# Rows of a routed expert layer turned by DMA transposes instead of by TensorE, from a scratch tensor kept as planes of 16-bit halves

## The chip, the cores and the metric

The kernel runs on one core of a Trainium2 chip, in one launch. The metric is device time in microseconds (us), the median of several executions; less is better. The core has TensorE (PE: matmuls, and PEld, its weight loads), VectorE (DVE), ScalarE (ACT), GpSimd (POOL), SyncE (SP, which here only issues transfers) and 16 DMA engines, which serve the transfers of all queues. SBUF is the working memory of 128 partitions, PSUM the memory of eight banks into which TensorE writes, HBM the main memory. Each engine takes its instructions in order.

## The reference

```python
X = np.fft.rfft(x, axis=1)                   # x: (8, 2496, 256) float32
y = np.fft.irfft(X * (filt_r + 1j * filt_i)[None], n=2496, axis=1)
x = y.reshape(19968, 256)                    # the 19,968 rows
logits = x @ w_gate
noisy = logits + np.log1p(np.exp(x @ w_noise)) * noise
top2 = np.argpartition(-noisy, 2, axis=1)[:, :2]     # 2 of 8 experts for each row
top2_w = softmax of the two noisy logits
for e in range(8):
    for k in range(2):
        mask = top2[:, k] == e
        h = np.maximum(x[mask] @ w1[e], 0.0)         # 256 -> 1024
        out[mask] += top2_w[mask, k, None] * (h @ w2[e])   # 1024 -> 256
```

## The kernel before, in words

The work has two streams that one program interleaves. `fft_stream` filters the eight batches one after the other, as matmuls with small DFT matrices (steps `s1`, `kg0` to `kg2`, `t3`, `i2`), and finds the two experts of each row and their weights (`gate`, `route`). Its last step `i2` (L505 on) brings a chunk of 4 groups of rows by 128 columns from PSUM to the tile `yt` with an ACT copy (L524) and writes it to the scratch tensor `y` in HBM with a DMA on SP's queue (L528). A row of `y` has 256 float32 values and 8 weights, one for each expert.

`expert` (L1069 on) takes the rows in parts of up to 512, all of one expert. For a part, `gather` (L985) fetches the rows from `y` with indirect DMAs on POOL's queue, 128 rows at a time (L993), into one of eight slots `xg` of the tile `stage`. `turn` (L999) turns them, so that the 256 columns lie on partitions: four TensorE transposes of 128 x 128 for each of the two column halves, with the identity as the moving operand, into the PSUM bank `xps` (L1009). ACT rounds the result to a coarse part `mxh` (L1013), DVE computes the rest `mxl` (L1014). The products are made from such pairs, coarse times coarse plus two mixed terms. The first layer is eight groups `f` of six matmuls of 512 columns (L121 to L123, into a bank of tag `hps`, every third one of tag `yps`); ACT and DVE make the pair `hh`, `hl` of each group (L1096, L1097). The second layer goes by row tiles `t` of 128, 16 matmuls each into a bank of tag `yps` (L1121 and L1122 with both halves of the weights side by side, once the batches are far enough, else L121 to L123); ACT and DVE scale the result (L1126, L1128), and an indirect DMA on POOL's queue adds it to `out` (L1129). The weights come by DMAs on SP's queue (`load_w`, L1030 for most) into four slots, and are split into pairs by ACT and DVE (`wsplit`, L1058, L1059). `front` starts the loads of a new expert's weights and calls `turn`.

The order of a part: first layer; then `turn` of the next part, whose rows were fetched by then; then the four tiles of the second layer, with `fetch` ahead of them for the part after the next. So the transposes stand between first and second layer on TensorE, which the FFT steps fill as well. `run` sets how many FFT steps go between the parts (`PACE`, `PACES`). The parts come in sets, one for each batch that is ready: `FIRST` counts parts with weights of their own (2 in all after the first batch, 12 after the second), `PAIRS` pairs of parts that share the weights (1, 6, 11, 16, 21, 26 in all after batches 3 to 8). At the end stand 7 single parts, 14 parts of 256 rows and 4 of 128. This makes 89 parts with 316 row tiles in the run. `pin` writes down the order of the instructions of some steps on their engines; the rest is ordered by the compiler's own schedule. The first two batches are filtered by a plan of slots (`plan`, in `fft_stream`), in which the `i2` of the first batch stand in slots 12 to 17.

## Time and profile before

| | |
|---|---|
| time, median of 3 runs | 2307.39 us (2306.23 to 2309.88) |
| profiled execution, its own time | 2308.6 us |
| its span in the trace | 2306.8 us |
| granted TensorE clock in it | 0.993 |
| TensorE matmul busy | 2253.9 us |
| DVE / ACT / POOL busy | 1540.0 / 1183.1 / 925.5 us |
| bytes moved by DMA | 328.58 MB |

The profile lists instructions by line of the kernel, engine and operation, with the tile written and the tiles read (`xps<-ident,stage` is a transpose of gathered rows into the bank `xps`), how often it ran, how long it was busy in all and in the mean, and how long the engine idled before it and for whom. Records of matmuls overlap, since they are pipelined: what a matmul costs is read from the distance of starts in the timeline, not from its own length. The table of windows gives, for a stretch of time, the busy time of each engine with the number of instructions, then the granted clock (PEclk), the share of time in which the 16 DMA engines were busy, and the rate. The chain of work is followed back from the last instruction to what released it, step by step, and its shares say what the span consists of.

### The profile page before, as it was taken

What the parts mean: (1) busy time and instruction counts of PE and PEld (TensorE: products, weight loads), DVE (VectorE), ACT (ScalarE), POOL (GpSimd) and SP (SyncE); (2) the same over time, 40 slices, a digit from 0 to 9 for tenths busy, and PEclk for the clock granted to TensorE, in tenths of its full rate; (3) what the DMA queues carried; (4) which work ended last, traced back from release to release, by engine and by line L of the source; (5) the groups of instructions that cost most, each with busy time, mean ns of one, the idle gap of its engine ahead of it and who ended that gap; (6) DMA issues with size and microseconds to landing.
All of it is one profiled execution on the core that took longest, in us unless ns stands there. A gap on an engine that the chain in (4) does not pass through costs nothing.

```text
span 2306.8 us, 39164 instructions
## 1 busy us (share of the span) xinstructions
PE 2253.9 (98%) x13023; PEld 1888.2 (82%) x13023; DVE 1540.0 (67%) x3348; ACT 1183.1 (51%) x2369; POOL 925.5 (40%) x819
## 2 busy tenths in 40 slices
PE   8889999999999999999999999999999999999998
PEld 5448888888788888888888888888888888889997
DVE  4767797687669765875659655964444445557886
ACT  6655655654554554444544444444344444546775
POOL 4014253343334333443344433435454544444442
PEclk9989999999999999999999999999999999999999
DMA  8686757755655555454544553444444444657774
GB/s 239 178 255 188 199 141 195 177 149 135 171 137 126 140 140 129 103 144 118 118 114 106 137 142 85 91 99 89 96 92 91 90 98 105 149 138 233 218 215 130
DMA packets 283957, 328.58 MB, mean 142 GB/s; under 512 B 37243, under 2 KB 196963, under 8 KB 283747
## 3 DMA queue, kind: packets, MB, share of 16 engines
q1 hardware_dynamic: 222435, 241.60, 34.5%
q0 software_dynamic: 61312, 84.40, 21.6%
q8 instruction: 104, 1.70, 0.3%
q14 instruction: 106, 0.87, 0.1%
HBM read 221.44 MB, written 105.25 MB: 142 GB/s over the span
## 4 chain that ended last, share of the span: by engine, by line
PE 89%; DMA 4%; DVE 3%; ACT 2%; issue 1%; SPq 1%; POOL 0%; POOLq 0%; ACTq 0%; DVEq 0%
PE yps L1121 21%; PE hps L121 12%; PE hps L122 12%; PE hps L123 12%; PE yps L1122 10%; PE xps L1009 3%; PE q L428 2%; PE yps L123 2%; PE yps L121 2%; PE yps L122 2%; PE q L492 1%; PE u L439 1%; DMA stage<-w 1%; DMA x<-x 1%; PE q L317 1%
## 5 line engine op out<-in xcount | busy, mean ns | idle before, releaser
L1121 PE MATMUL yps<-w,hh 128*128 128x512 f32 x2080 | 737.6, 399 | 0.6 <-DVE stage L1128 0.6
L1129 POOL DMA_INDIRECT out<-stage,ids x316 | 524.8, 1661 | 291.2 <-DVE stage L1128 116.9
L993 POOL DMA_INDIRECT stage<-y,ids x316 | 324.0, 1025 | 623.7 <-PE xps L1009 247.1
L1122 PE MATMUL yps<-w,hl 128*128 128x256 f32 x2080 | 563.3, 280 | 0.1
L1097 DVE SCALAR_TENSOR_TENSOR hl<-hps,hh 128x512 fp32r<-128x512 f32 (+2 forms) x712 | 435.0, 626 | 153.7 <-ACT hh L1096 151.9
L122 PE MATMUL hps<-mxl,w1h 128*128 128x512 f32 (+2 forms) x1424 | 533.0, 375 | 0.0
L121 PE MATMUL hps<-mxh,w1h 128*128 128x512 f32 (+2 forms) x1424 | 524.1, 378 | 1.7 <-DVE hl L1097 1.4
L123 PE MATMUL hps<-mxh,w1l 128*128 128x512 f32 (+2 forms) x1424 | 525.0, 370 | 0.0
L1096 ACT ACTIVATE hh<-hps 128x512 fp32r<-128x512 f32 (+2 forms) x712 | 377.7, 550 | 247.2 <-PE hps L123 241.7
L1121 PEld LDWEIGHTS yps<-w,hh 128*128 128x128 f32 x2080 | 384.2, 188 | 80.4 <-DVE stage L1128 0.9
L1122 PEld LDWEIGHTS yps<-w,hl 128*128 128x128 f32 x2080 | 391.1, 188 | 19.9 <-DVE mxl L1014 1.2
L121 PEld LDWEIGHTS hps<-mxh,w1h 128*128 128x128 f32 x1424 | 265.1, 188 | 50.5 <-DVE hl L1097 3.7
L123 PEld LDWEIGHTS hps<-mxh,w1l 128*128 128x128 f32 x1424 | 268.4, 188 | 45.5
L122 PEld LDWEIGHTS hps<-mxl,w1h 128*128 128x128 f32 x1424 | 268.3, 188 | 40.4 <-issue 0.2
L1126 ACT ACTIVATE stage<-yps,gt 128x256 f32<-128x256 f32 x316 | 142.3, 476 | 281.1 <-PE yps L1122 256.7
L1128 DVE SCALAR_TENSOR_TENSOR stage<-yps,gt,stage 128x256 f32<-128x256 f32 x260 | 119.4, 479 | 184.5 <-ACT stage L1126 184.1
L1014 DVE TENSOR_TENSOR mxl<-xps,mxh 128x512 fp32r<-128x512 f32 (+2 forms) x178 | 112.1, 630 | 149.1 <-ACT mxh L1013 147.0
L1013 ACT CAST mxh<-xps 128x512 fp32r<-128x512 f32 (+2 forms) x178 | 95.9, 539 | 203.3 <-PE xps L1009 170.3
L1058 ACT CAST w1h<-stage 128x512 fp32r<-128x512 f32 x180 | 111.8, 621 | 99.8 <-PE hps L122 52.1
L1059 DVE TENSOR_TENSOR w1l<-stage,w1h 128x512 fp32r<-128x512 f32 x180 | 123.7, 687 | 55.5 <-ACT w1h L1058 54.6
L965 POOL CAST ids<-lt 128x8 int32<-128x8 f32 (+3 forms) x63 | 16.2, 257 | 336.2 <-DMA lt<-lst 330.1
L1059 DVE TENSOR_TENSOR w<-stage,w 128x512 fp32r<-128x512 f32 x216 | 142.4, 686 | 7.9 <-ACT w L1058 7.4
(222 smaller groups left out, 3082.4 us busy)
## 6 DMA issues: line engine op xcount, KB each, us to landing
stage<-w SPq DMA_DIRECT2D x396, 256.0 KB
x<-x SPq DMA_DIRECT2D x88, 256.0 KB
fd<-c SPq DMA_DIRECT2D x77, 240.0 KB
wb<-w SPq DMA_DIRECT2D x18, 1024.0 KB
fx<-fd SPq DMA_DIRECT2D x140, 128.0 KB
out<-z SPq DMA_DIRECT2D x24, 702.0 KB
y<-yt SPq DMA_DIRECT2D x40, 248.6 KB
y<-yt SPq DMA_DIRECT2D x40, 234.0 KB
```

The lines of the kernel that those rows point to most:

```text
L121: nc.tensor.matmul(o, lh, rh, start=start, stop=False)
L122: nc.tensor.matmul(o, lh, rl, start=False, stop=False)
L123: nc.tensor.matmul(o, ll, rh, start=False, stop=stop)
L993: self.pin(lambda: self.nc.gpsimd.indirect_dma_start(out=x, out_offset=None, in_=self.y[:BLK + ready * ROWS], in_offset=bass.IndirectOffse ...
L1059: nc.vector.tensor_sub(l, sv, f32v(h))
L1096: nc.scalar.activation(h, p, AF.Relu)
L1097: nc.vector.scalar_tensor_tensor(l, p, 0.0, f32v(h), op0=ALU.max, op1=ALU.subtract)
L1121: nc.tensor.matmul(bank, h, hl, start=(f == 0), stop=False)
L1122: nc.tensor.matmul(p, l, hl[:, 0], start=False, stop=(f == 7))
L1126: nc.scalar.activation(o, p, AF.Copy, scale=gate[:, t])
L1128: nc.vector.scalar_tensor_tensor(o, bank[:, 1], gate[:, t], o, op0=ALU.mult, op1=ALU.add)
L1129: a = nc.gpsimd.indirect_dma_start(out=self.io["out"][:BLK + ready * ROWS], out_offset=bass.IndirectOffsetOnAxis(ap=ids[:, t:t + 1], axis= ...
```

## The change

- `y` becomes a tensor of 32-bit words in which each 128-column half of a row is stored as 128 low 16-bit halves and then 128 high ones. In `i2`, the ACT copy from PSUM to `yt` goes by 16-bit halves and sorts them so (1024 elements per partition and chunk in place of 512). For the first batch the float32 rows go as before to a tensor `y0` of their own, and POOL makes the planes in a second tile `yp` (tags of `x` and `a`); `yput` writes those to `y`, 12 chunks and one transfer of the weights, in the slots of the plan ahead of the next `i2`. `init_dram` zeroes the pad rows of `y0` too.
- Parts of the set after the first batch (2 parts, 8 row tiles) are gathered from `y0` and turned by TensorE as before. All later parts are gathered from `y`, and `flip` turns each row tile with one DMA transpose of 128 x 512 16-bit elements on SP's queue, into the tile `xt`. `flip` is called after group `f == 1` of the first layer (what is left), and after the second and the fourth tile of the second layer (two row tiles each; all that are there for smaller parts), each time scheduled behind the ACT instruction just issued. `turn` then has two DVE copies of 2 x 512 16-bit elements that put the halves together again as float32 in two slots `x32`, ordered behind the last `hl` of the first layer; L1013 and L1014 follow, and read SBUF in place of PSUM.
- The weights of the rows (`gt`, a POOL copy) are taken when a part's transposes have been issued (`take`), no longer in `turn`. The slots `xg` are 4 in place of 8, those of the scaled results 4 in place of 6. A next part is fetched ahead of the first layer only if the one before it has been flipped.
- The third bank of the first layer has the tag `xps` in place of `yps` for all parts but those of the first set.
- `FIRST` becomes 2, 12, 16: after the third batch four single parts in place of one pair. `PAIRS` becomes 4, 9, 14, 19, 24 after batches 4 to 8. The number of parts stays 89. `PACE` of that third set is 60 in place of 40, and the stream may run a batch further ahead in it.
- The tiles `uh` and `oh` of the gating share buffers with others.

```diff
-FIRST = [_sure(2 * S, BLK), 12]
+FIRST = [_sure(2 * S, BLK), 12, 16]
+ALONE = len(FIRST)
...
-PACE = {0: 110, 1: 200, 2: 40}
+PACE = {0: 110, 1: 200, 2: 60}
...
-        self.y = self.dp.tile([NROW, YW], F32, name="y")
+        self.y = self.dp.tile([NROW, YW], I32, name="y")
+        self.y0 = self.dp.tile([BLK + ROWS, YW], F32, name="y0")
...
+        if n < 2:
+            nc.scalar.copy(yt[:, :k, :128], p[:RP, :m].rearrange("p (g d) -> p g d", g=k))
+            y0 = self.y0[BLK:].rearrange("(p g) d -> p g d", p=RP)[:, g0:g0 + k]
+            nc.sync.dma_start(y0[:, :, h * 128:h * 128 + w], yt[:, :k, :w])
+            yp = P.tile([RP, 4, 128], F32, name="yp", tag="xa"[g0 // 4 % 2], bufs=2)
+            nc.gpsimd.tensor_copy(yp.bitcast(U16)[:, :k].rearrange("p g (two d) -> p g two d", two=2),
+                                  yt.bitcast(U16)[:, :k, :256].rearrange("p g (d two) -> p g two d", two=2))
+            self.yp.append((y[:, :, h * 128:h * 128 + 128], yp.bitcast(I32)[:, :k]))
...
+        nc.scalar.copy(yt.bitcast(U16)[:, :k, :256].rearrange("p g (two d) -> p g two d", two=2),
+                       p.bitcast(U16)[:RP, :2 * m].rearrange("p (g d two) -> p g two d", g=k, two=2))
+        nc.sync.dma_start(y[:, :, h * 128:h * 128 + w], yt.bitcast(I32)[:, :k, :w])
...
+    def flip(self, count, late=None):
+        ent = next((e for e in self.ahead if len(e[3]) < len(e[2][0])), None)
+        if ent is None or ent[0][5] == 1 or self.standing not in (None, ent):
+            return
+        self.standing = ent
+        xg, done = ent[2][0], ent[3]
+        if not done:
+            ent[4] = self.P.tile([128, 4, 512], U16, name="xt", bufs=1)
+        with self.after(late):
+            for t in range(len(done), min(len(done) + count, len(xg))):
+                done.append(self.nc.sync.dma_start_transpose(ent[4][:, :, 128 * t:128 * t + 128], xg[t].bitcast(U16)[:, :2 * D]))
+        if len(done) == len(xg):
+            ent[5] = self.take(ent)
...
+        if ent[0][5] > 1:
+            self.flip(nt)
+            q = [self.slot("x32") for _ in range(2)]
+            for kc in range(2):
+                with self.after(self.lastl):
+                    nc.vector.tensor_copy(q[kc].bitcast(U16)[:, :2 * w].rearrange("p (t two) -> p two t", two=2), ent[4][:, 2 * kc:2 * kc + 2, :w])
+            self.standing = None
...
+            third = ("xps", 1) if ready > 1 else ("yps", 2)
...
+                if f == 1:
+                    self.flip(4, e)
...
+                if t % 2 or nt == 1:
+                    self.flip(2 if nt == 4 else 4, e)
```

More of the change, by code (lines that the diff above doesn't have):

```diff
@@ L615, in fft_stream @@
                     at(o, self.t3, *R[i + 1])
+                if b == 0 and (i == 0 or o > last):
+                    at(o, self.yput)
+                last = o
                 at(o, self.i2, *R[i])
+            if b == 0:
+                at(o + 1, self.yput)
         for j in range(11):
@@ L980, in front @@
             fill()
-        if fill and self.held_any:
-            xT = self.pin(self.turn, xg, nt, hold=False, only=[self.nc.tensor.engine])
+        if fill and self.held_any and ready == 1:
+            xT = self.pin(self.turn, ent, hold=False, only=[self.nc.tensor.engine])
         else:
-            xT = self.turn(xg, nt)
+            xT = self.turn(ent)
         return w1, xT, w2st
     def gather(self, blk, i):
+        nc = self.nc
         lt, n, nt, s, tabi, ready = blk
+        if i == 0:
+            self.ra = nc.gpsimd.value_load(tabi[0:1, 1, s:s + 1], min_val=0, max_val=E - 1)
         xg = []
@@ L992, in gather @@
             x = self.slot("xg")
-            self.pin(lambda: self.nc.gpsimd.indirect_dma_start(
-                out=x, out_offset=None, in_=self.y[:BLK + ready * ROWS],
+            o, y = (x, self.y0) if ready == 1 else (x.bitcast(I32), self.y[:BLK + ready * ROWS])
+            self.pin(lambda: nc.gpsimd.indirect_dma_start(
+                out=o, out_offset=None, in_=y,
                 in_offset=bass.IndirectOffsetOnAxis(ap=lt[:, i, t:t + 1], axis=0)),
-                hold=False, only=[self.nc.gpsimd.engine])
+                hold=False, only=[nc.gpsimd.engine])
@@ L997, in gather, with take @@
             xg.append(x)
-        return xg, self.turns["xg"] + 1 - nt
-    def turn(self, xg, nt):
-        nc, P = self.nc, self.P
+        return xg, self.turns["xg"] + 1 - nt, self.ra
+    def take(self, ent):
+        xg, at, ra = ent[2]
+        gate = self.P.tile([128, 4, 1], F32, name="gt", bufs=3)[:, :len(xg)]
+        rows = self.stage[:, 2048:2048 + 4 * YW].rearrange("p (s w) -> p s w", w=YW)[:, at:at + len(xg), D:]
+        self.nc.gpsimd.tensor_copy(gate, rows[:, :, bass.ds(ra, 1)])
+        return gate
@@ L1005, in turn @@
-        w = 128 * nt
         for kc in range(2):
-            q = self.PS.tile([128, 512], F32, name="xps", bufs=1)
-            for t in range(nt):
-                nc.tensor.transpose(q[:, t * 128:(t + 1) * 128], xg[t][:, kc * 128:(kc + 1) * 128], self.ident)
+            if ent[0][5] > 1:
+                x = q[kc]
+            else:
+                x = self.PS.tile([128, 512], F32, name="xps", bufs=1)
+                for t in range(nt):
+                    nc.tensor.transpose(x[:, t * 128:(t + 1) * 128], xg[t][:, kc * 128:(kc + 1) * 128], self.ident)
@@ L1084, in expert @@
             ids, gate = lt[:, i], xT[2]
-            self.fetch(may)
+            if not self.ahead or len(self.ahead[0][3]) == len(self.ahead[0][2][0]):
+                self.fetch(may)
+            third = ("xps", 1) if ready > 1 else ("yps", 2)
             hh = []
             for f in range(8):
-                p = self.PS.tile([128, 512], F32, name="hps", tag="hps" if f % 3 < 2 else "yps", bufs=2)[:, :w]
+                tag, bufs = ("hps", 2) if f % 3 < 2 else third
+                p = self.PS.tile([128, 512], F32, name="hps", tag=tag, bufs=bufs)[:, :w]
                 for kc in range(2):
@@ L1105, in expert @@
             if self.ahead:
-                b2, i2, x2 = self.ahead[0]
-                cur = (w1, self.turn(x2, nt), None) if i2 else self.front(b2, x2, fill if late else None)
+                e2 = self.ahead[0]
+                cur = (w1, self.turn(e2), None) if e2[1] else self.front(e2, fill if late else None)
             self.fetch(may)
```

78 lines of the change are left out of this document (43 added, 35 removed).

## Prediction

> **What bounds the kernel now.** I read the page first (which engine fills the span), then the chain of waits, then the table of windows, and last the timeline of a stretch without FFT work, for what the transposes cost there.
>
> ```profile
> span 2306.8 us, 39164 instructions
> PE 2253.9 (98%) x13023; PEld 1888.2 (82%) x13023; DVE 1540.0 (67%) x3348; ACT 1183.1 (51%) x2369; POOL 925.5 (40%) x819
> ...
> PE 89%; DMA 4%; DVE 3%; ACT 2%; issue 1%; SPq 1%; POOL 0%; POOLq 0%; ACTq 0%; DVEq 0%
> PE yps L1121 21%; PE hps L121 12%; PE hps L122 12%; PE hps L123 12%; PE yps L1122 10%; PE xps L1009 3%; PE q L428 2%; PE yps L123 2%; PE yps L121 2%; PE yps L122 2%; PE q L492 1%; PE u L439 1%; DMA stage<-w 1%; DMA x<-x 1%; PE q L317 1%
> ```
>
> TensorE is the bound: 98% busy, 89% of the chain. The transposes of rows (L1009) are 3% of the chain, 0.03 x 2306.8 = 69 us. In the middle of the run nothing else is near:
>
> ```profile
> 1600.00:1700.00 100.00, 100.00 (x524) 84.55 (x523) 46.78 (x78) 40.15 (x77) 45.49 (x42) 1.00 0.42 90
> ```
>
> Here PE is busy for 100 us of 100, DVE for 46.8, ACT for 40.2, POOL for 45.5, and the DMA engines for a share of 0.42. Work taken from TensorE shortens such a stretch one for one, until another of these fills.
>
> **The transposes that go.** Starts tell the price:
>
> ```profile
> 1675.75 0.39 PE L123 MATMUL hps<-mxh,w1l 128*128 128x512 f32 x1
> ...
> 1675.98 0.60 PE L1009 MATMUL xps<-ident,stage 128*128 128x128 f32 x4
> 1676.33 0.48 PE L1121 MATMUL yps<-w,hh 128*128 128x512 f32 x1
> 1676.65 0.28 PE L1122 MATMUL yps<-w,hl 128*128 128x256 f32 x1
> 1676.77 0.40 PE L1121 MATMUL yps<-w,hh 128*128 128x512 f32 x1
> 1677.00 0.28 PE L1122 MATMUL yps<-w,hl 128*128 128x256 f32 x1
> ...
> L1009 PE MATMUL xps<-ident,stage 128*128 128x128 f32 x632 | 101.5, 274 | 14.2 <-DMA stage<-y,ids 12.7 <-DVE mxl L1014 1.4
> ```
>
> Four transposes hold TensorE from 1675.98 to 1676.33, 0.35 us, or 0.0875 us each. The matmul behind them takes 0.32 us to the next start instead of 0.23 (1676.77 to 1677.00), which makes 0.11 each; the chain's 69 us over 632 is 0.11 too. The first two parts keep 2 x 4 x 2 = 16 of the 632, so 616 go: 616 x 0.0875 = 54 us at least, 616 x 0.11 = 68 at most. I take 65, near the value on which two views agree. A full part has 48 matmuls of 0.23 and 32 of 0.23 and 0.12 by turns, 11.0 + 11.2 = 22.2 us, and with eight transposes 23.1.
>
> **DVE, the two copies of each part.** The rounding pair counts parts:
>
> ```profile
> L1014 DVE TENSOR_TENSOR mxl<-xps,mxh 128x512 fp32r<-128x512 f32 (+2 forms) x178 | 112.1, 630 | 149.1 <-ACT mxh L1013 147.0
> L919 DVE TENSOR_TENSOR oc<-half,lo 117x512 f16<-117x512 f16 x88 | 53.4, 617 | 0.0
> L917 DVE TENSOR_TENSOR oc<-half,hi 117x224 f16<-117x224 f16 x88 | 30.1, 354 | 3.4 <-PE ra L922 2.9 <-DVE rx L926 0.2
> 300.00:325.00 25.00, 25.00 (x168) 22.93 (x167) 23.70 (x78) 15.07 (x30) 12.60 (x11) 1.00 0.59 139
> 325.00:350.00 25.00, 24.87 (x184) 21.75 (x183) 23.86 (x51) 10.95 (x22) 13.49 (x9) 1.00 0.64 172
> 1225.00:1250.00 25.00, 24.36 (x128) 20.36 (x127) 23.73 (x74) 10.01 (x19) 11.10 (x10) 1.00 0.56 135
> 2150.00:2175.00 25.00, 25.00 (x178) 23.23 (x177) 20.55 (x42) 17.92 (x43) 12.20 (x13) 1.00 0.73 212
> ```
>
> 178 rounds are two for each of 89 parts; 174 copies come in. No row shows a strided 16-bit copy. The two 16-bit groups give (617 - 354) / 288 = 0.91 ns an element, so 1024 elements take 617 + 512 x 0.91 = 1.08 us, 2.2 a full part; half of it would do if DVE took two at a time, twice if the stride cost. With 69 full parts, 14 halves and 4 quarters I get about 170 us more DVE, 1540 to 1710: not the bound in the mean. In the second layer, 11 us long, the two copies and the rounding find room. Where the routing of a batch runs, DVE is busy 23.7 to 23.9 us of 25 already, and one part's 2.2 more would make it 26: about 1 us late in each of two such windows a batch. For six later batches and a little of the tail (20.6 + two half parts of 1.2 = 23.0 of 25) that is 8 us between 0 (the schedule moves it) and 40 (doubled price).
>
> **ACT and POOL, the planes.**
>
> ```profile
> L524 ACT COPY yt<-q 117x512 f32<-117x512 f32 x96 | 52.9, 551 | 36.1 <-PE q L518 25.7 <-PE q L514 7.4 <-DMA y<-yt 1.4
> L526 ACT COPY yt<-dense 117x32 f32<-117x32 f32 (+1 forms) x48 | 10.6, 222 | 3.3 <-DVE dense L781 2.5 <-DMA y<-yt 0.8
> L415 POOL TENSOR_TENSOR ab<-ab 128x512 f32<-128x512 f32 x10 | 12.7, 1267 | 11.3 <-DVE ab L414 11.3
> 50.00:100.00 50.00, 41.62 (x189) 23.37 (x188) 32.92 (x129) 31.47 (x64) 0.00 (x0) 0.90 0.64 179
> 100.00:150.00 50.00, 36.90 (x198) 20.94 (x196) 34.83 (x111) 27.30 (x52) 10.57 (x13) 0.86 0.78 250
> ```
>
> By L524 and L526 an element costs ACT 0.69 ns, so a chunk of 1024 takes 0.90 us, 0.35 more, in 84 chunks 29 us; ACT has 1100 us free. Nothing on the path. POOL's 12 copies cost at least L415's 1.27 us each, up to twice that, and lie in 50 to 100 us, where POOL does nothing at all. The first batch is written twice: 2574 rows of 1056 bytes, 2.7 MB. In 100 to 150 us the engines move 250 GB/s at a share of 0.78, 320 at full share, so this is 8.5 us of all engines, in a stretch where TensorE idles for a quarter of the time and gathers are on the chain; SP has 13 more issues there, each behind POOL's copy, and the loads and writes of the plan behind those. Cost 0 to 8.5; I take 3, since most of these writes come before the list that the first gather waits for.
>
> **The DMA transposes.** 316 - 8 = 308 of 128 KB each:
>
> ```profile
> q1 hardware_dynamic: 222435, 241.60, 34.5%
> q0 software_dynamic: 61312, 84.40, 21.6%
> stage<-y,ids POOLq DMA_INDIRECT x316, 2.8
> out<-stage,ids POOLq DMA_INDIRECT x316, 4.5
> SPq L1030 <- DVE w1l L1059: 535.1, 136, 19.1
> ```
>
> No transfer here transposes. At the rate just used one would hold the engines for 131 KB / 320 = 0.4 us; the gather of the same rows lands in 2.8 us with all its latency, the adding scatter in 4.5. I take 1.5 us as occupancy, between the rate and the gather: 308 x 1.5 = 460 us, the two queues' share goes from 56% to 76%. They are due late: the pairs stand behind tiles two and four of the second layer, and the part needs them only at the end of its predecessor's first layer, 11 us later. So I cost them at nothing on the path. Cover fails when engine time exceeds what is free: at a share of 0.42, 58 us of 100 are free, and 100 us hold 100 / 23.1 = 4.3 parts, or 17.3 transposes, so 3.35 us each. On SP, the weight loads (L1030) queue behind a transpose that waits for its rows; SP waits 535 us in all for DVE's splits anyway, so it has slack, but order can cost. I allow 3 us for it, from 0 to 0.5 us a part, 45 us. A next part fetched too late at the border of two sets would put its transposes in `turn`, in the open; the fetch rule keeps two parts ahead, so nothing for that.
>
> Here the Trainium skill disagrees with itself. "VectorE: DVE Perf Modes" (section on the three transpose paths) gives a DMA transpose of 128 x 128 16-bit elements 1309 ns against 390 on TensorE; four of them per instruction would be 5.2 us, above the 3.35 us, and the steady part would be DMA-bound. "Advanced Engine Details and Errata" (X-Bar Transpose) calls them as fast as other DMAs, at which the sum stays. No run here shows it.
>
> **The third set.**
>
> ```profile
> 500.00:600.00 100.00, 92.65 (x617) 81.54 (x619) 72.57 (x176) 44.88 (x91) 39.59 (x30) 0.98 0.55 140
> ```
>
> This is the only stretch after 150 us in which TensorE visibly idles, 7.35 us: the one pair after the third batch has a batch's FFT to hide. Four single parts in its place spread that, at two more sets of weights (4 MB; 16 more splits on ACT and DVE). I take 3 us back, from -3 to 7. The own bank `xps` for each third group costs nothing: its transposes are gone.
>
> **Sum.** 2308.6 - 65 + 8 (DVE) + 3 (start) + 3 (SP's order) - 3 (third set) = 2254.6. The median is 1.2 below the profiled execution, so 2253; I round to 2255.
>
> **Rivals.** (1) The DMA engines become the bound, and it is slower. For it: 0.42 is the lowest share of the run, and 87 of 89 parts would carry transposes. Against it: 131 KB moves in 0.4 us at plain rate. It decides from 3.35 us each. At 4 us, a steady part needs 0.42 x 23.1 + 16 = 25.7 us of engine time against 23.1 now, +2.6, and over the 70 or so full parts 180 us: about 2490. Just past the point, at 3.5 us, it is 9.7 + 14.0 = 23.7, +0.6, 40 us: 2350. The slow end of the skill's prices is this rival. (2) The gain is eaten by order: SP's 45 us, DVE's 40 us in whole or part, so 2308.6 - 65 + 45 to 85, about 2288 to 2328; it needs the transposes or copies to stand ahead of what TensorE waits for next. In the tail a half part is short (11.9 us by the windows' 0.23 / 2 scale), and the weight loads share the ring there, at a DMA share of 0.73. (3) The transposes do not leave the path: flipped in `turn`, each part adds gather-like landing time, 2.8 us or more, less 0.88 of transposes, 87 x 1.9 = 165 us: 2475; FFT steps would fill part of it in the first two thirds. (4) More than forecast: 68 on TensorE, 7 in the third set, nothing elsewhere: 2233.
>
> **How the numbers follow.** The forecast, 2235 to 2285, has 0.57; rival 2 0.16, of which 0.05 falls within 0.2% of before (2303 to 2312, about what a measurement can tell from no change) and 0.04 above; rival 1 0.16; rival 3 0.06; rival 4 0.05. Faster: 0.57 + 0.05 + 0.07 = 0.69; same 0.05; slower 0.04 + 0.16 + 0.06 = 0.26. The range leaves out half of rival 4 and the far ends of 1 and 3: 2234 to 2345; the likeliest case alone is 2235 to 2285.
>
> **What would show it.** Right: L1009 left with 16, steady parts of about 22.3 us between first groups, two DVE copies of about 1.1 us a part, DMA share near 0.6 in 1600 to 1700, no idle time of TensorE behind them. Wrong: TensorE waiting for `mxh`, `mxl` or for weights, transposes that land later than 11 us after issue, a DMA share near 1, DVE at 25 of 25 us for long, or a first gather later than 125 us.

## The result: slower, 2362.86 us, and the profile after

| | before | after |
|---|---|---|
| time, median | 2306.81 us (2305.04 to 2309.88, 4 runs) | 2362.86 us (2357.92 to 2367.49, 4 runs) |
| profiled execution, its own time | 2308.6 us | 2357.92 us |

The ratio is 1.0244, 95% interval 1.0231 to 1.0256: 56 us slower. The forecast was 2255, its range 2234 to 2345. The times before in this table are those taken beside the changed kernel.

The page of the changed kernel, engines first, then the chain of waits:

```profile
span 2356.1 us, 39048 instructions
...
PE 2231.1 (95%) x12471; PEld 1838.7 (78%) x12471; DVE 1645.6 (70%) x3530; ACT 1231.2 (52%) x2385; POOL 974.6 (41%) x833
...
PE 62%; DVE 8%; ACT 3%; issue 2%; DMA 2%; SPq 1%; DVEq 0%; POOL 0%; ACTq 0%; POOLq 0%
PE yps L1191 17%; PE hps L124 10%; PE hps L123 10%; PE hps L125 9%; PE yps L1192 8%; DVE stage L1066 2%; PE q L431 1%; DVE w L1124 1%; ACT w1h L1123 1%; DVE hl L1165 1%; PE q L495 1%; DVE w1l L1124 1%; DMA stage<-w 1%; ACT hh L1164 1%; DVE stage L1198 1%
```

TensorE is less busy than before by 23 us in a span that is 49 us longer, so it idles. DVE's share of the chain went from 3% to 8%, and the copies (L1066) have a line of their own there: 2%, 47 us. Before, no line of DVE was among those listed. The shares of this second chain add up to 78%, since it could be followed back only to about 530 us; so its 62% of TensorE can't be set against the 89% of before as they stand.

What was forecast of the parts, from the groups, the queues and the tile `xt`:

```profile
L1066 DVE COPY stage<-xt 128x1024 uint16<-128x1024 uint16 (+2 forms) x174 | 107.9, 677 | 0.0
...
L543 ACT COPY yt<-q 117x1024 uint16<-117x1024 uint16 x84 | 79.2, 944 | 39.6 <-PE q L521 33.3 <-PE q L517 5.2 <-DMA y<-yt 0.5
...
L535 POOL COPY yp<-yt 117x1024 uint16<-117x1024 uint16 (+1 forms) x12 | 12.8, 1068 | 35.2 <-ACT yt L531 27.4 <-DVE oc L947 5.4 <-DMA y<-yp 2.4
...
L1075 PE MATMUL xps<-ident,stage 128*128 128x128 f32 x16 | 3.7, 303 | 2.5 <-DMA stage<-y,ids 2.4
```

```profile
q1 hardware_dynamic: 400742, 289.47, 45.9%
q0 software_dynamic: 61312, 84.40, 21.9%
```

```profile
L1051 SPq DMA_TRANSPOSE xt<-stage x308: 1188/1248/2962, 208.8 to 2326.3; - x154
```

16 transposes are left on TensorE, as forecast. The copies are cheaper than forecast (107.9 us in all, not 170), ACT's planes cost 0.94 us a chunk (forecast 0.90). So no single operation is much dearer than expected; the DMA transposes take SP's queue for 1.25 us each, and SP's queue q1 went from 34.5% to 45.9% of the engines.

The window of the changed kernel that answers to that of before:

```profile
1600.00:1700.00 100.00, 96.74 (x485) 80.78 (x484) 49.52 (x82) 39.83 (x74) 49.17 (x43) 1.00 0.61 115
```

In 1600 to 1700, where PE was busy for 100.00 us of 100, it is now busy for 96.74. It has 485 matmul records in place of 524, of which some 35 were transposes (100 / 23.1 parts of eight), so there are no more matmuls of the layers than before. The DMA share is 0.61, about the forecast's 0.6, and DVE has half of the stretch free. No engine is full: something waits in order.

The timeline shows it, at the border between the first layer of one part and what follows (columns: start, length, engine, line; in square brackets the idle time before and who ended it):

```profile
1711.35 0.39 PE L125 MATMUL hps<-mxh,w1l 128*128 128x512 f32 x1
...
1712.82 0.68 DVE L1165 SCALAR_TENSOR_TENSOR hl<-hps,hh 128x512 fp32r<-128x512 f32 x1
...
1713.22 0.63 PE L1191 MATMUL yps<-w,hh 128*128 128x512 f32 x2
1713.42 1.36 DVE L1066 COPY stage<-xt 128x1024 uint16<-128x1024 uint16 x2
...
1713.69 0.40 PE L1192 MATMUL yps<-w,hl 128*128 128x256 f32 x2
1714.06 0.84 ACT L1196 ACTIVATE stage<-yps,gt 128x256 f32<-128x256 f32 x2 [1.39 <-issue]
1714.67 0.87 DVE L1198 SCALAR_TENSOR_TENSOR stage<-yps,gt,stage 128x256 f32<-128x256 f32 x2
1714.79 1.14 ACT L1079 CAST mxh<-stage 128x512 fp32r<-128x512 f32 x2
...
1715.19 0.50 PE L1191 MATMUL yps<-w,hh 128*128 128x512 f32 x1 [1.11 <-DVE stage L1198]
...
1715.44 1.29 DVE L1080 TENSOR_TENSOR mxl<-stage,mxh 128x512 fp32r<-128x512 f32 x2
```

At 1711.35 TensorE starts the last matmul of the first layer. The last residue of that layer ends at 1713.50; the two copies stand behind it and hold DVE until 1714.78. At 1713.69 TensorE starts the last two matmuls of two tiles of the second layer (x2, one for each), which so end at once. Both `yps` banks are then full, and the third tile has to wait until ACT (L1196) and DVE (L1198) have emptied one: TensorE stands until 1715.19. The next first layer could run in the meantime, but its input is not there. Copies, L1079 and L1080 come one behind the other, and ACT does the two evictions ahead of L1079.

DVE's half of the eviction stands behind the copies too, but this costs little. L1198 starts 0.61 us behind L1196 here (1714.06 to 1714.67); where DVE is free, in run e13 below, the same step starts 0.51 us behind. Most of the 1.11 us is the eviction itself, with nothing else for TensorE to do.

That tiles of the second layer run beside the first layer, and that two of them end together, is not new. The compiler's order mixes them so in the kernel before as well (in its trace L1122 and L1121 stand among the first layer's groups at 1690.28, and ACT evicts two tiles in a row at 1697.22), though the program writes the second layer behind the first.

The waits of TensorE over the whole run:

```profile
PE yps L1191 <- DVE stage L1198: 22.2, 21, 1.6
PE hps L123 <- ACT mxh L1079: 10.6, 29, 1.4
PE hps L124 <- DVE mxl L1080: 8.9, 18, 2.3
PE q L517 <- ACT yt L543: 8.7, 4, 4.3
```

The first three are waits of this kind at a part's border, the fourth is in the steps of `i2`. From 1550 us on there is no FFT work left to fill them; from there to the last full part the view gives:

```profile
PE yps L1191 <- DVE stage L1198: 16.7, 15, 1.1
PE hps L123 <- ACT mxh L1079: 4.6, 9, 0.5
```

So 15 of the 24 borders have the wait of 1.1 us for a bank, and the other nine one of 0.5 us for the rounding, behind the copies. The start shows in the first row of the first layer (first and last start of its matmuls), before and then after:

```profile
L121 PE MATMUL hps<-mxh,w1h x1424: 220/392/797, 161.5 to 2294.8; 128*128 128x512 f32 x142, 128*128 128x256 f32 x28, 128*128 128x128 f32 x8
```

```profile
L123 PE MATMUL hps<-mxh,w1h x1424: 221/392/797, 175.3 to 2344.0; 128*128 128x512 f32 x142, 128*128 128x256 f32 x28, 128*128 128x128 f32 x8
```

The first part begins 13.8 us later.

### The profile page after: what moved, and what is told of

It reads as the page before. It is cut to its first block, busy times and chain, and to the rows that moved or that the text cites. A ratio compares the mean times of both kernels' runs of the same rounds, so it can differ in the third digit from the quotient of the medians.

```text
span 2356.1 us, 39048 instructions
## 1 busy us (share of the span) xinstructions
PE 2231.1 (95%) x12471; PEld 1838.7 (78%) x12471; DVE 1645.6 (70%) x3530; ACT 1231.2 (52%) x2385; POOL 974.6 (41%) x833
## 2 busy tenths in 40 slices
DMA packets 462269, 376.45 MB, mean 160 GB/s; under 512 B 207842, under 2 KB 373222, under 8 KB 462054
## 3 DMA queue, kind: packets, MB, share of 16 engines
q1 hardware_dynamic: 400742, 289.47, 45.9%
## 4 chain that ended last, share of the span: by engine, by line
PE 62%; DVE 8%; ACT 3%; issue 2%; DMA 2%; SPq 1%; DVEq 0%; POOL 0%; ACTq 0%; POOLq 0%
PE yps L1191 17%; PE hps L124 10%; PE hps L123 10%; PE hps L125 9%; PE yps L1192 8%; DVE stage L1066 2%; PE q L431 1%; DVE w L1124 1%; ACT w1h L1123 1%; DVE hl L1165 1%; PE q L495 1%; DVE w1l L1124 1%; DMA stage<-w 1%; ACT hh L1164 1%; DVE stage L1198 1%
## 5 line engine op out<-in xcount | busy, mean ns | idle before, releaser
L1191 PE MATMUL yps<-w,hh 128*128 128x512 f32 x2016 | 701.1, 400 | 25.5 <-DVE stage L1198 22.2
L1199 POOL DMA_INDIRECT out<-stage,ids x316 | 529.8, 1676 | 423.8 <-DVE stage L1198 212.7
L123 PE MATMUL hps<-mxh,w1h 128*128 128x512 f32 (+2 forms) x1424 | 506.5, 380 | 17.3 <-ACT mxh L1079 10.6
L1025 POOL DMA_INDIRECT stage<-y,ids x316 | 343.4, 1087 | 409.0 <-DMA xt<-stage 250.5
L1192 PE MATMUL yps<-w,hl 128*128 128x256 f32 x2016 | 508.0, 281 | 1.2 <-DVE hl L1165 1.2
L1191 PEld LDWEIGHTS yps<-w,hh 128*128 128x128 f32 x2016 | 355.5, 188 | 94.0 <-DVE stage L1198 26.1
L1192 PEld LDWEIGHTS yps<-w,hl 128*128 128x128 f32 x2016 | 373.8, 189 | 37.4 <-DVE hl L1165 4.2
L123 PEld LDWEIGHTS hps<-mxh,w1h 128*128 128x128 f32 x1424 | 259.7, 189 | 74.8 <-ACT mxh L1079 17.3
L1196 ACT ACTIVATE stage<-yps,gt 128x256 f32<-128x256 f32 x316 | 142.1, 475 | 229.2 <-PE yps L1192 180.9
L1198 DVE SCALAR_TENSOR_TENSOR stage<-yps,gt,stage 128x256 f32<-128x256 f32 x252 | 115.2, 477 | 139.0 <-ACT stage L1196 138.2
L994 POOL CAST ids<-lt 128x4 int32<-128x4 f32 (+3 forms) x65 | 33.3, 512 | 408.2 <-DMA lt<-lst 408.0
L1124 DVE TENSOR_TENSOR w<-stage,w 128x512 fp32r<-128x512 f32 x224 | 152.2, 689 | 31.9 <-ACT w L1123 27.6
L123 PE MATMUL yps<-w,hh 128*128 128x256 f32 x512 | 145.8, 289 | 10.5 <-ACT hh L1164 8.2
L1123 ACT CAST w<-stage 128x512 fp32r<-128x512 f32 x224 | 137.5, 624 | 27.1 <-PE yps L1192 17.4
```

What stands on the lines that cost most here:

```text
L123: nc.tensor.matmul(o, lh, rh, start=start, stop=False)
L1025: self.pin(lambda: nc.gpsimd.indirect_dma_start(out=o, out_offset=None, in_=y, in_offset=bass.IndirectOffsetOnAxis(ap=lt[:, i, t:t + 1], a ...
L1123: nc.scalar.copy(h, sv)
L1124: nc.vector.tensor_sub(l, sv, f32v(h))
L1191: nc.tensor.matmul(bank, h, hl, start=(f == 0), stop=False)
L1192: nc.tensor.matmul(p, l, hl[:, 0], start=False, stop=(f == 7))
```

## The experiments

The theory after this reading: with the own bank `xps`, two tiles of the second layer go in step beside the first layer, one in each `yps` bank, and end soon behind it; then the copies are late for the evictions and the rounding, and TensorE stands. Rivals: the DMA transposes cost the time (engine time, or SP's queue); DVE's load costs it wherever the copies stand; the late start is the larger part. All ratios are to the kernel before on the same chip; 0.01 is 23 us.

**What the gain could be: e1_before_no_turn, e5_before_third_set.** The first is the kernel before without TensorE's transposes:

```diff
-            q = self.PS.tile([128, 512], F32, name="xps", bufs=1)
-            for t in range(nt):
-                nc.tensor.transpose(q[:, t * 128:(t + 1) * 128], xg[t][:, kc * 128:(kc + 1) * 128], self.ident)
+            q = self.stage[:, 2048:2048 + 8 * YW].rearrange("p (s w) -> p s w", w=YW)[:, at:at + nt, kc * 128:(kc + 1) * 128]
...
```

> The kernel before, with the 632 TensorE transposes left out: the rounding reads the gathered rows as they lie (so rows are not turned, and what the layers multiply is not the row). Theory A, the price was right and the new waits of the change eat it: 2307 - 65 = about 2242 us, 2235 to 2255. Theory B, the transposes stood where TensorE would wait anyway, for the rounding or for a bank to be read out: at least half of the 65 us stays, 2275 to 2307 us, with TensorE idle at the border of the layers.

Measured: 2260.09 us, ratio 0.9781 (0.9760 to 0.9801): 51 to 52 us. This is between the ranges of the two theories, near the first. The forecast's 65 for this term was somewhat high.

The second is the kernel before with `FIRST`, `PAIRS` and `PACE` of the change:

```diff
-FIRST = [_sure(2 * S, BLK), 12]
+FIRST = [_sure(2 * S, BLK), 12, 16]
...
-PACE = {0: 110, 1: 200, 2: 40}
+PACE = {0: 110, 1: 200, 2: 60}
...
```

> The kernel before with the third set alone: FIRST 2, 12, 16 with the later pairs, PACE 60 and the longer lead of the stream, and nothing else of the change. The prediction's term: 3 us less, from -7 to +3 against before. Rival: four more sets of single weights in the stretch where DVE is fullest cost 5 to 15 us.

Measured: 2310.02 us, ratio 0.9989 (0.9978 to 1.0): about 3 us better (0 to 5), as forecast.

**Which addition costs: e2_after_no_dma_turn, e3_after_no_merge, e4_after_third_yps.** Each takes one thing out of the changed kernel. First the 308 DMA transposes (the copies then read the gathered rows):

```diff
-                done.append(self.nc.sync.dma_start_transpose(ent[4][:, :, 128 * t:128 * t + 128], xg[t].bitcast(U16)[:, :2 * D]))
+                done.append(t)
...
```

> The changed kernel with the 308 DMA transposes left out: the two DVE copies read the gathered rows directly, with as many elements and the same strides (so rows are not turned). Theory C, the transposes on SP's queue delay the other transfers and the rows: 2363 falls by 40 us or more, to 2325 or less. Theory B, the waits come from the order of the layers and the banks: 2345 to 2365, and TensorE still waits about 1.1 us for L1198 at the border of the layers in 1600 to 2000 us.

Measured: 2343.46 us, ratio 1.0133 (1.0113 to 1.0153), still slower than before. They are worth 0.0111, 26 us, a quarter of what separates 1.0244 from 0.9781. But the waits at the borders from 1550 to 2117 us stay as they were:

```profile
PE yps L1194 <- DVE stage L1201: 16.7, 15, 1.1
```

So the DMA transposes do not make them. SP's queue without them:

```profile
q1 hardware_dynamic: 233190, 249.06, 35.5%
```

45.9% of 2356.1 less 35.5% of 2347.1 us is 248 us of all 16 engines, 0.81 us for each transpose. Second, the 174 copies on DVE:

```diff
-            q = [self.slot("x32") for _ in range(2)]
-            for kc in range(2):
-                with self.after(self.lastl):
-                    nc.vector.tensor_copy(q[kc].bitcast(U16)[:, :2 * w].rearrange("p (t two) -> p two t", two=2), ent[4][:, 2 * kc:2 * kc + 2, :w])
+            q = [ent[4][:, 2 * kc + 1] for kc in range(2)]
```

> The changed kernel with the 174 DVE copies left out: the rounding reads the plane of high halves as numbers (so the rows' values are others). Theory D, the copies ahead of L1198 and L1080 on DVE make TensorE wait for the bank and for the rounding: most of the waits at the borders go, 2363 falls by 30 to 60 us. If they are harmless, under 10 us. Theory B alone: the wait of 1.1 us stays, as its chain has L1164, L1165, L1196 and L1198 in it.

Measured: 2287.37 us, ratio 0.9898 (0.9876 to 0.9919): 80 us better than the changed kernel, more than the 30 to 60 expected, for an operation of 108 us on an engine that was 70% busy. Third, the own bank:

```diff
-            third = ("xps", 1) if ready > 1 else ("yps", 2)
+            third = ("yps", 2)
```

> The changed kernel with every third group of the first layer in a bank of tag yps again, as before the change, for all parts. Theory B, with the own bank two tiles of the second layer run beside the first layer and end together, so that TensorE waits for the eviction of both: the 1.1 us at the borders goes, 2363 falls by 15 to 40 us. If the bank is harmless: within 5 us of the changed kernel, or slower, as a bank is given up.

Measured: 2301.44 us, ratio 0.9959 (0.9945 to 0.9972): 66 us better than the changed kernel, again more than expected, with all copies and all DMA transposes in place. A border in this run:

```profile
1691.06 0.40 PE L125 MATMUL hps<-mxh,w1l 128*128 128x512 f32 x1
...
1693.12 1.39 DVE L1066 COPY stage<-xt 128x1024 uint16<-128x1024 uint16 x2
...
1693.96 1.26 ACT L1079 CAST mxh<-stage 128x512 fp32r<-128x512 f32 x2 [1.58 <-DVE stage L1066]
...
1695.06 0.40 PE L1192 MATMUL yps<-w,hl 128*128 128x256 f32 x2
1695.30 0.62 PE L123 MATMUL hps<-mxh,w1h 128*128 128x512 f32 x2
...
1695.42 0.84 ACT L1196 ACTIVATE stage<-yps,gt 128x256 f32<-128x256 f32 x2 [0.20 <-PE yps L1192]
```

Here too two tiles end together, and the copies stand behind the last residue. But from the last matmul of the first layer to the last pair of the two tiles TensorE has 4.0 us of second layer left (1691.06 to 1695.06), against 2.3 in the changed kernel (1711.35 to 1713.69). That covers copies and rounding: the next first layer starts at 1695.30, and the evictions run beneath it. From 1550 to 2117 us the view of waits has no line for TensorE. The copies of 150 us in the middle, in the changed kernel and then in this one (count, min/median/max in ns, first and last start):

```profile
L1066 DVE COPY stage<-xt x12: 728/742/753, 1619.9 to 1737.4; 128x1024 uint16<-128x1024 uint16 x12
```

```profile
L1066 DVE COPY stage<-xt x14: 747/750/754, 1603.5 to 1738.6; 128x1024 uint16<-128x1024 uint16 x14
```

Two copies belong to a part, the second 0.6 us behind the first. So a part takes (1737.4 - 1619.9 - 0.6) / 5 = 23.4 us in the changed kernel, and (1738.6 - 1603.5 - 0.6) / 6 = 22.4 with the old bank, where the forecast had 22.3.

These parts are not the whole of it. The next rows give the first and the last start of the first layer's matmuls from the 48th part to the start of the 73rd, and from there to the start of the 87th (nearly all parts of 256 rows), each time in the changed kernel and then in e4:

```profile
L123 PE MATMUL hps<-mxh,w1h x401: 277/394/503, 1550.9 to 2135.3; 128*128 128x512 f32 x128, 128*128 128x256 f32 x6
L123 PE MATMUL hps<-mxh,w1h x225: 222/280/388, 2135.3 to 2316.5; 128*128 128x256 f32 x104, 128*128 128x128 f32 x9
```

```profile
L123 PE MATMUL hps<-mxh,w1h x401: 277/391/406, 1538.5 to 2093.0; 128*128 128x512 f32 x128, 128*128 128x256 f32 x6
L123 PE MATMUL hps<-mxh,w1h x225: 222/280/388, 2093.0 to 2252.2; 128*128 128x256 f32 x104, 128*128 128x128 f32 x9
```

Of the 64 us between the two traces, 12 have come up by the 48th part (1550.9 against 1538.5), where FFT work still fills TensorE; 30 come in the next 25 parts (584.4 against 554.5), 1.2 a part; and 22 in the 14 short parts behind them (181.2 against 159.2), 1.6 a part. The listed waits make up 21 of the 30. In the short parts the waits for L1079 and L1080 come to 8 us (from 2117 us on); the rest of the 22 was not traced.

**The copies earlier: e6_after_early_merge.** The bank stays; the copies are issued after group 5, ordered behind the residue of group 4:

```diff
+                ll = nc.vector.scalar_tensor_tensor(l, p, 0.0, f32v(h), op0=ALU.max, op1=ALU.subtract)
+                self.lastl = ll if f < 5 else self.lastl
...
+                if f == 5 and self.ahead and len(self.ahead[0][3]) == len(self.ahead[0][2][0]):
+                    self.merge(self.ahead[0])
...
```

> The changed kernel, with the third groups in the bank xps as the change has them, but the two DVE copies ordered behind the rest of group five of the first layer in place of group eight, where the next part's rows have been turned by then. Theory D, what costs is the copies' 1.4 us between the last hl and the eviction L1198: the waits of 1.3 and 0.7 us at the borders go and 2363 falls by 40 us or more, with the bank left as it is. Theory B, it is the bank: 2350 or more.

Measured: 2293.80 us, ratio 0.9912 (0.9896 to 0.9929): 77 us better than the changed kernel, with bank, copies and DMA transposes all there.

**The table of four: e9_third_yps_no_merge.** Both edits of e4 and e3 together.

> The changed kernel with third groups back in `yps` and without DVE's 174 copies: the rounding reads the turned halves as they lie, so the numbers in `xt` are wrong ones. With this, the two suspects stand in a table of four: bank and copies (2363), bank without copies (2287), no bank with copies (2301), and this one, neither. Theory of the border (the copies cost only where the own bank lets two second-layer tiles end together with the first layer, so that the copies lie between the last residue and the eviction): the copies are nearly free here, 2285 to 2300. Rival, each costs by itself (the copies by DVE's time, the bank by the order): the two gains add, 2363 - 76 - 62 = 2225, at least below 2250.

Measured: 2269.39 us, ratio 0.9841 (0.9824 to 0.9857).

| | copies | no copies | the copies cost |
|---|---|---|---|
| own bank | 1.0244 | 0.9898 | 80 us |
| old bank | 0.9959 | 0.9841 | 27 us |
| the bank costs | 66 us | 13 us | |

Both expectations missed. The copies are not nearly free with the old bank, and the two gains do not add: 53 us belong to bank and copies together. The 27 us that the copies cost with the old bank stand in the traces before 1540 us, where the FFT and the routing run (the 48th part starts at 1538.5 in e4 and at 1511.6 in e9); from there on both take 22.4 to 22.5 us a part. Whether it is DVE's load there or the order was not settled.

**Wait or order: e13_after_copies_unread, e14_after_copies_on_pool.** All these edits also change the compiler's order. So two runs keep the bank, and the first keeps DVE's work as well, but nobody reads the copies:

```diff
+            q = [ent[4][:, 2 * kc + 1] for kc in range(2)]
```

> The changed kernel with its own bank and all 174 copies on DVE, at the same place in DVE's order (behind the last residue, ahead of the evictions of the second layer), but nothing reads them: the rounding takes the turned halves as they lie, so the numbers in `mxh` and `mxl` are wrong ones. Theory A, it is DVE's time at the border (the evictions stand behind 1.4 us of copies): the stall stays, 2335 to 2365. Theory B, it is the chain: the copy stands between the first layer's end and the rounding on which the next first layer waits, and with that longer chain the compiler's order leaves two second-layer tiles to end together: without the chain the stall goes although DVE still does the copies, 2280 to 2300, like the run without copies (0.99 of before).

Measured: 2299.47 us, ratio 0.9937 (0.9916 to 0.9957). The timeline at the same place:

```profile
1711.67 0.62 ACT L1080 CAST mxh<-xt 128x512 fp32r<-128x512 uint16 x1 [0.55 <-PE hps L125]
...
1713.01 0.69 DVE L1166 SCALAR_TENSOR_TENSOR hl<-hps,hh 128x512 fp32r<-128x512 f32 x1
...
1713.61 1.38 DVE L1066 COPY stage<-xt 128x1024 uint16<-128x1024 uint16 x2
1713.81 0.40 PE L1193 MATMUL yps<-w,hl 128*128 128x256 f32 x2
...
1714.04 0.63 PE L123 MATMUL hps<-mxh,w1h 128*128 128x512 f32 x2
...
1716.72 0.84 ACT L1197 ACTIVATE stage<-yps,gt 128x256 f32<-128x256 f32 x2 [3.24 <-issue]
...
1717.23 0.88 DVE L1199 SCALAR_TENSOR_TENSOR stage<-yps,gt,stage 128x256 f32<-128x256 f32 x2 [1.67 <-ACT stage L1197]
```

The copies stand where they stood, behind the last residue, but TensorE goes on with the next first layer (L123): its `mxh` does not wait for them, and is made from 1711.67 on, ahead of the copies. The two tiles that end together are evicted later (L1197, L1199), beneath the next first layer. DVE's 1.4 us at the border alone cost about 0.0039, 9 us, against e3, with intervals that overlap. The second run moves the copies to POOL, and was to leave them in the chain:

```diff
-                    nc.vector.tensor_copy(q[kc].bitcast(U16)[:, :2 * w].rearrange("p (t two) -> p two t", two=2), ent[4][:, 2 * kc:2 * kc + 2, :w])
+                    nc.gpsimd.tensor_copy(q[kc].bitcast(U16)[:, :2 * w].rearrange("p (t two) -> p two t", two=2), ent[4][:, 2 * kc:2 * kc + 2, :w])
```

> The changed kernel with its own bank, and the 174 copies on GpSimd instead of DVE; the output is the same. DVE is free at the border, the chain copy, rounding, first layer stays. Theory A (DVE's time): the stall goes, 2285 to 2300. Theory B (the chain and the order that it gives): the chain is at least as long, as POOL's copy of 1024 halves took 1.07 us against 0.68 on DVE, and the next first layer waits for it: 2340 to 2400. If the order is as in the run without copies and the second-layer tile is long enough to cover POOL, 2290 too, and then the bank itself is harmless.

Measured: 2298.99 us, ratio 0.9930 (0.9913 to 0.9946).

```profile
L1066 POOL COPY stage<-xt x174: 477/1356/2759, 222.2 to 2270.2; 128x1024 uint16<-128x1024 uint16 x138, 128x512 uint16<-128x512 uint16 x28, 128x256 uint16<-128x256 uint16 x8
```

A copy takes 1.36 us here, 0.74 on DVE, and yet the stall is gone. But this is not the longer chain that the run was to test, as the timeline shows:

```profile
1706.20 0.62 ACT L1079 CAST mxh<-stage 128x512 fp32r<-128x512 f32 x1 [0.61 <-PE hps L125]
...
1707.34 0.61 ACT L1079 CAST mxh<-stage 128x512 fp32r<-128x512 f32 x1
...
1707.61 1.36 POOL L1066 COPY stage<-xt 128x1024 uint16<-128x1024 uint16 x1 [1.10 <-DVE mxl L1080]
...
1709.53 1.34 POOL L1066 COPY stage<-xt 128x1024 uint16<-128x1024 uint16 x1 [0.56 <-DVE mxl L1080]
```

Both roundings of this border (L1079) start before the copies of this border. Each copy here starts when the residue L1080 of the part before has freed its slot `x32`, and the rounding that reads it comes one border later: here the pair at 1706.20 and 1707.34 reads copies that started at 1685.29 and 1687.60. On POOL the copies so went a part ahead, by chance of the order, and the run is one more in which the rounding need not wait at the border. What a longer chain would cost was not tested.

So the runs agree on two conditions. The own bank leaves less of the second layer behind the first (2.3 us in place of 4.0), and the rounding of the next part stands behind copies that start only when the first layer is done. The old bank takes away the first (e4); no copies (e3), early copies (e6), unread copies (e13) and copies a part ahead (e14) take away the second. Where one of the two is missing, the stall is gone: from 1550 to 2117 us the view of waits lists at most 4 us for TensorE in each of these five runs, against 22 in the changed kernel. That DVE also evicts is no condition: in e13 it does the copies in the same place.

**The start, and cleaner versions: e7, e8, e10, e11, e12, e15.** In the changed kernel ACT copies the dense weights into `yt` ahead of the rows (L529) and waits there 58.7 us in all for earlier writes of `yt`. The kernel before copied them behind the rows (L526); the list of the change does not name this. The run e7_third_yps_dense_last is e4 with that copy behind the copy from PSUM, in both branches of `i2`:

```diff
-        if h:
-            nc.scalar.copy(yt[:, :k, 128:], self.dense[:, g0:g0 + k])
...
+        if h:
+            nc.scalar.copy(yt[:, :k, 128:], self.dense[:, g0:g0 + k])
```

> The kernel of e4 (third groups in yps), with the copy of the rows' weights into yt written behind the copy from PSUM, as before the change. Theory E, this copy, which needs nothing of TensorE, comes first and holds ACT until the write of yt has landed (58.7 us of idle in the changed kernel), and TensorE waits for q: 5 to 20 us less than e4, most of it before the first part and in the first set. Rival: ACT has slack, within 3 us of e4.

Measured: 2281.86 us, ratio 0.9864 (0.9847 to 0.9880), 22 us better than e4. The first part begins at 173.3 us, only 2.5 earlier, so that most of the gain comes later, not before the first part as expected.

The run e8_third_yps_zero_y is e4 without POOL's 12 copies; the writes send zeros:

```diff
-            yp = P.tile([RP, 4, 128], F32, name="yp", tag="xa"[g0 // 4 % 2], bufs=2)
-            nc.gpsimd.tensor_copy(...)
-            self.yp.append((y[:, :, h * 128:h * 128 + 128], yp.bitcast(I32)[:, :k]))
+            self.yp.append((y[:, :, h * 128:h * 128 + 128], self.z.bitcast(I32)[:RP, :128].unsqueeze(1).to_broadcast([RP, k, 128])))
```

> The kernel of e4, with POOL's 12 copies of the first batch left out; yput writes zeros from a constant tile in the same places (so the rows of the first batch are zero in all sets but the first). The transfers stay, the waits on POOL go. Theory F, yput's wait on POOL holds SP's queue in the start: the first part starts up to 14 us earlier and the time falls by as much. Rival, the start is later for ACT's longer copies or for the added bytes: within 3 us of e4.

Measured: 2294.23 us, ratio 0.9914 (0.9897 to 0.9930), 10 us better than e4; the first part begins at 170.5, 5.3 us earlier than in e4.

The run e10_after_early_dense is e6 with e7's edit; e11_third_yps_early_dense has the old bank besides.

> The changed kernel with its own bank for third groups kept, two edits of order: the copies are put ahead of the last group of the first layer (as in the run that gave 2294), and ACT's copy of the dense weights into the planes of y stands behind the copies of the transposed rows instead of ahead of them. Theory that the start is a cost of its own (ACT held by the first batch's row writes behind the dense copy): the two gains add, 2294 - 20 = 2274, between 2265 and 2285, and the first part begins at about 173 us. Rival, that the late dense copy only helped through another order of the second layer: no gain with the bank, 2290 to 2298.

Measured: 2282.95 us, ratio 0.9900 (0.9883 to 0.9916). Against e6's 0.9912 that is no difference the intervals can tell, as the rival had it, and the first part begins at 176.5, not at 173.

> Third groups in `yps`, copies put ahead of the last group of the first layer, dense weights copied last. Theory of the border: with the old bank nothing waits for the copies, so that putting them early brings nothing more, 2278 to 2286, as without it (2282). Rival, that the copies still cost TensorE some tenths of a microsecond at each border with the old bank, in the tail above all (some 0.3 us of 89 borders): 2250 to 2270.

Measured: 2272.12 us, ratio 0.9842 (0.9819 to 0.9864), against 0.9864 without the early copies; the two intervals overlap. This is the fastest median of the runs that leave nothing out: by the ratios 36 us faster than before and 93 faster than the change.

The run e12_dense_last_no_dma_turn is e7 with e2's edit.

> Third groups in `yps`, dense weights copied last (2282), and the 308 DMA transposes left out: the copies read the gathered rows as they are, so the numbers in `xt` are wrong ones. Theory that the DMA transposes are cheap on the path: 2268 to 2282, 0 to 14 us below the run with them. Rival, that what is left of the 52 us that leaving TensorE's transposes out can bring (2260 against 2313) is lost to the DMA transposes, in engine time or in SP's order: 2255 to 2262.

Measured: 2273.22 us, ratio 0.9863 (0.9842 to 0.9885), against 0.9864 with the transposes: no difference, within some 5 us. The middle of the run, in e7 and then in e12:

```profile
1600.00:1700.00 100.00, 100.00 (x498) 83.85 (x497) 54.47 (x89) 42.60 (x79) 50.88 (x44) 1.00 0.58 123
```

```profile
1600.00:1700.00 100.00, 100.00 (x505) 84.13 (x504) 54.88 (x91) 42.91 (x80) 51.38 (x45) 1.00 0.42 94
```

PE is busy throughout in both. The DMA share falls by 0.16 to the 0.42 of before; with 100 / 22.4 x 4 = 17.9 transposes in the window that is 0.9 us of all engines each.

The run e15_early_dense_y_zeroed is e11 without the second writing of the first batch; one early DMA of zeros stands for it:

```diff
-            self.yp.append((y[:, :, h * 128:h * 128 + 128], yp.bitcast(I32)[:, :k]))
...
+    def zero_y(self):
+        y = self.y[BLK:BLK + ROWS].rearrange("(p g) d -> p g d", p=RP)
+        self.nc.sync.dma_start(y, self.z.bitcast(I32)[:RP].unsqueeze(1).to_broadcast([RP, NG, YW]))
```

> Third groups in `yps`, early copies, dense weights last (2272), with the second writing of the first batch taken out of the first blocks' steps: POOL's 12 copies and 13 writes are gone, and one DMA writes zeros there early, so that later parts gather zeros for the first batch's rows. Theory that the late start (first part at 175.6 against 161.5 us before) comes from this writing: the first part starts at 162 to 168 and the time falls by as much, 2258 to 2266. Rival, that the start is late through the DMA transposes or the compiler's order: first part at 172 or later, 2268 to 2276.

Measured: 2263.88 us, ratio 0.9778 (0.9762 to 0.9794). The rows of the first layer in e12 and then in e15:

```profile
L123 PE MATMUL hps<-mxh,w1h x1424: 222/391/795, 169.3 to 2256.8; 128*128 128x512 f32 x142, 128*128 128x256 f32 x28, 128*128 128x128 f32 x8
```

```profile
L123 PE MATMUL hps<-mxh,w1h x1424: 220/391/797, 172.1 to 2246.0; 128*128 128x512 f32 x142, 128*128 128x256 f32 x28, 128*128 128x128 f32 x8
```

A mixed answer: the first part begins at 172.1 in place of e11's 175.6, 3.5 us and not 8 to 14, as the rival had it, while the time falls by 0.0064, 15 us, as the theory had it or more. The rest came later in the run, and was not traced. The shares of the start don't add up cleanly. Taking out the dense copy gives 2.5 (175.8 in e4 to 173.3), the second writing 3.5 here but POOL's copies alone 5.3 (e8). The 4.0 us of e12 (173.3 to 169.3) can't be time of the DMA transposes, of which the first is issued at 208.8 us, but only another order. So of the 13.8 us of the start some 6 to 8 have a cause; the rest was not settled.

## Why the prediction was wrong

The steps of the sum and what the runs give for each, in us at 2307 for 1.0:

| step | forecast | measured |
|---|---|---|
| transposes off TensorE | -65 | -51 (e1) |
| DVE's copies | +8 | +27 with the old bank (e9 to e4) |
| own bank for third groups | 0 | +66 (e4 to the change) |
| start | +3 | +14 (first part; not a run's difference) |
| SP's order, DMA transposes | +3 | 0 (e7 to e12) |
| third set | -3 | -3 (e5) |

The column on the right sums to +53, the change is +56. But the table of four shows that rows two and three are one thing for the most part, and each pair of kernels differs in order too, so that a single row is good to some 10 us, and the close sum is in part luck.

**The step that failed** is "The own bank `xps` for each third group costs nothing: its transposes are gone", with the step that it upsets, "In the second layer, 11 us long, the two copies and the rounding find room". The first counted the bank's owners and saw that it was free. It did not ask what the two `yps` banks would be used for once the first layer left them. Two tiles of the second layer then went in step beside the first layer, and too little of them was left to cover copies and rounding: 2.3 us in place of 4.0. At 1713.69 the last matmuls of both tiles start, and TensorE waits until 1715.19. The room of 11 us was never there in one piece, since the compiler runs part of the second layer beside the first, before the change too; and the rounding is due not anywhere in it, but before the next first layer. The prediction's own list had the sign of it: "TensorE waiting for `mxh`, `mxl`". With the old bank a part takes 22.4 us, nearly the forecast's number.

**The price of the copies** was too high for one (1.08 against 0.74 us). For its DVE term the prediction's own working, six batches with two windows of 1 us each, gives 12, not 8; with the old bank the copies cost 27, inside its range of 0 to 40, and where it put them, before the FFT's end. What it missed is the stall. The rival "eaten by order" named the condition rightly (copies "ahead of what TensorE waits for next") and then bounded it by DVE's time, 40 us. The price of a wait in order is the idle time of TensorE at each border where no other work fills it, here 0.5 or 1.1 us, and that was not bounded.

**TensorE's gain** was mis-sized: 51 in place of 65. The lower end of the working, 54, was nearer. In the trace of e1, 31 us of the gain have come up by the 48th part, 23 come in the next 25 parts, 0.9 each as forecast, and 1 in all behind them; why the short parts gain so little was not traced.

**The start** was taken at 3 of 0 to 8.5 us, by bandwidth. Measured is 13.8, of which the second writing is some 3.5 to 5.3 (e15, e8); the order of ACT's copies and of SP's queue was not in the sum.

**The DMA transposes** cost nothing on the path, as forecast (e12), and the rival of full DMA engines fell. They take 0.8 us of the engines by the queue (e2), 0.9 by the window (e12); forecast were 1.5, and the limit 3.35. In the changed kernel they still cost 26 us (e2), which vanishes in e7 to e12; the waits at the borders are the same without them, and why else they weigh there was not traced. The prediction's "0.42 is the lowest share of the run" was a misreading (1200 to 1225 us had 0.35), on which nothing turned.

The Trainium skill's "VectorE: DVE Perf Modes" (three transpose paths) gives 1309 ns for 128 x 128; an estimate of 5.2 us from it, for four blocks one after another, is not borne out for this 128 x 512 transpose. The Trainium skill's "Advanced Engine Details and Errata" (X-Bar Transpose) calls transposing DMAs as fast as regular ones. That is nearer but too low: a plain transfer of 131 KB at the 320 GB/s that the prediction worked out is 0.41 us, half of what was measured.

**What stays open.** Why the compiler put the two tiles in step beside the whole first layer in the changed kernel and not with the old bank. No run kept its order and changed the wait only, so the stall is shown by the timeline, by the view of waits and by five edits that each remove it (bank, no copies, early copies, copies unread, copies on POOL), not by one edit at a fixed order. Open are also the 12 us that bank and order cost before the 48th part, most of the 22 us of the short parts, and about half of the late start.

## What to carry to other kernels

When an edit frees a buffer or a PSUM bank, ask what the schedule will start in it, and whether that work was the cover of something else: here the second layer was to hide the copies, and the free bank let too much of it run early. Work added between two matmul stages should be ordered ahead of the last instruction of the earlier one (e6), so that the next stage's input is ready when the earlier one ends. And a term bounded by an engine's busy time does not bound a wait in order: that bound is the idle time of the engine that sets the pace, times the number of borders at which nothing else is left to run. Last, an edit can do something else than it was meant to: here the copies on POOL had left the chain.

## What the runs showed of the hardware

A DMA transpose of 128 x 512 16-bit elements held SP's queue for 1.25 us, took 0.8 to 0.9 us of the 16 engines, and came with 544 packets (167552 / 308), so that the packets of the run rose from 283,747 (the two queues before) to 462,054, with no loss of time that e7 and e12 could tell (0.9864 and 0.9863, each to 0.002). A strided 16-bit copy of 1024 elements a partition took 0.74 us on DVE, 0.94 on ACT from PSUM and 1.36 on POOL. That is 0.72 ns an element on DVE, where the groups of before had suggested 0.91.
